# Moving the clamp of the weight decoding to GpSimd, one piece ahead, and the bonus product to VectorE

## The chip, the cores and the metric

One core of a Trainium2 chip runs the whole program. The metric is device time in microseconds (us) of one execution, the median over several. Engines are named as in the profile: PE is TensorE (PEld its weight loads), DVE is VectorE, ACT is ScalarE, POOL is GpSimd, SP is SyncE, which here only issues DMAs.

## The reference

The program is a linear attention with decay followed by two feed-forward mixers, for batch B=4, H=8 heads of D=48, S=768 steps, in fp32:

```python
cur = einsum('bhd,bhe->bhde', u[None] * kt, vt)      # bonus of the own step
y[:, :, t] = einsum('bhd,bhde->bhe', rt, state + cur)
state = w[None, :, :, None] * state + einsum('bhd,bhe->bhde', kt, vt)
...
h = maximum(x @ w_in, 0);  gate = sigmoid(conv3(h, conv_w))   # mixer 1, 384 -> 1024 -> 384
x = (h * gate) @ w_out
x + maximum(layernorm(x) * g_ln @ w_ch1, 0) @ w_ch2            # mixer 2, 384 -> 1536 -> 384
```

The weights of both mixers (w_in, conv_w, w_out, w_ch1, w_ch2) arrive as 64-bit floats, `x` of a mixer is fp32.

## The kernel before, in words

**Attention.** It works on 24 tiles of 128 steps (`attn_tile`, six a batch). A tile's keys are first multiplied by decay factors and by the bonus `u` in one DVE product (`decayed_k`, L224), which is issued two tiles ahead. Transposes on PE give `rT` (DVE L248) and `kT` (ACT L253). The bonus term of a step is the sum over d of r times k times u: the product `av` (L256, on POOL before), its sum by head `a8` (L258, DVE), and a diagonal matrix `aT` made from it by an `affine_select` (L261, POOL). Then `copy_predicated` (L271, DVE) puts the other scores of PE's `dps` into `aT`, PE makes `yps`, and L294 and L295 split it into a rounded part (ACT) and a rest (DVE). `state_update` carries the state on (L322, L324, L325 on DVE, L328 and L329 on ACT).

**Mixers.** Work goes by 8 blocks `j` of 384 steps. Every matmul of the mixers is three fp32r products (high by high, high by low, low by high). Mixer 1 has 8 slices `f` a block, with gate work on DVE (L377, L383, L396) and ACT; mixer 2 has 12 slices a block. All eight blocks of mixer 1 come first, with the attention tiles they need fed in between by `pace` (`after1`); their results go to DRAM and come back for mixer 2.

**Weight decoding.** The 22 pieces of weights (`wjobs`) come in an order written out: 0 to 2 and 4 to 6 are the halves of w_in, 512 wide; 3 and 7 to 9 are w_out, 10 to 15 w_ch1, 16 to 21 w_ch2, all 768 wide. A piece's 64-bit words are loaded by an SP DMA to `st` (three buffers), one piece ahead (`wload`). The decoding (`decode`) takes the magnitude of the high word on ACT, clamps it on DVE (`tensor_scalar` with max and min), shifts it (`tensor_scalar`), and merges the low word and then the sign (two `scalar_tensor_tensor`, "stt" below); then ACT writes the rounded part (`wih`, `woh`, `c1h`, `c2h`), and DVE the rest (`wil`, `wol`, `c1l`, `c2l`). The result of the decoding is the tile `wdec`, two buffers. All of it is recorded on line L70, that of the helper `InOrder`, which holds the operations of an engine that go through it in program order; what doesn't go through it is placed by a scheduler that plans with its own model of times.

**When a piece is decoded.** `decode` and `steps` are generators; `wdo` takes steps from them. Before, a piece has four steps with a pause behind each, and the last subtraction is joined to the next piece's first. In the start-up (four attention tiles) two steps follow each half tile, up to piece 2; in block j=0 two steps follow each of 16 slots; in j=1 to 5 every third slot has a step, in j=6 and 7 every second; in mixer 2 two steps follow each slice. `need` forces a piece to be done before the slice that uses it: in j=0 pieces 4 to 6 before f=4 and piece 7 two slices behind.

Of the kernel before, what the change touches and what calls it, by code (L numbers as in the profile page):

```python
# [8 lines left out]
F32 = mybir.dt.float32  # L9
F32R = mybir.dt.float32r  # L10
I32 = mybir.dt.int32
AF = mybir.ActivationFunctionType
ALU = mybir.AluOpType
AX = mybir.AxisListType

B, H, S, D = 4, 8, 768, 48
DM = H * D
# [3 lines left out]
NF1 = FF1 // 128  # L21
NF2 = FF2 // 128
# [21 lines left out]
def body(ctx, tc, r, k, v, w, u, w_in, conv_w, w_out, g_ln, w_ch1, w_ch2, out):  # L44
# [28 lines left out]
    vo = InOrder(nc.vector)  # L73
    ao = InOrder(nc.scalar)
    so = InOrder(nc.sync)


    ident = const.tile([128, 128], F32, name="ident")
# [25 lines left out]
    y_dram = dram.tile([B, S + 2, DM], F32, name="y_dram")  # L104


    def decode(st, n):

        words = st[:, 0:2 * n].rearrange("p (n two) -> p n two", two=2)
        lo, hi = words[:, :, 0], words[:, :, 1]  # L110
        t = ap.tile([128, WN], F32, tag="wd", name="wdec", bufs=2)[:, 0:n]
        ti = t.bitcast(I32)
        ao.activation(out=t, in_=hi.bitcast(F32), func=AF.Abs)
        vo.tensor_scalar(out=t, in0=t, scalar1=W_MIN, scalar2=W_MAX, op0=ALU.max, op1=ALU.min)
        yield
        vo.tensor_scalar(out=ti, in0=ti, scalar1=5, scalar2=2, op0=ALU.logical_shift_left,
                         op1=ALU.logical_shift_right)
        yield
        vo.scalar_tensor_tensor(out=ti, in0=lo, scalar=29, in1=ti, op0=ALU.logical_shift_right, op1=ALU.bitwise_or)
        yield  # L120
        vo.scalar_tensor_tensor(out=ti, in0=hi, scalar=-(2 ** 30), in1=ti, op0=ALU.bitwise_and, op1=ALU.bitwise_or)
        return t

    wjobs = []

    def wjob(src, n, hi, lo, scale=None):

        st = []

        def load():  # L130
            st.append(io.tile([128, 2 * WN], I32, tag="st", name="st", bufs=3))
            dst = st[0][:, 0:2 * n]
            if len(src.shape) == 3:
                dst = dst.rearrange("p (a n) -> p a n", a=src.shape[1])
            so.dma_start(out=dst, in_=src.bitcast(I32))

        def steps():
            t = yield from decode(st[0], n)
            if len(src.shape) == 3:
                t = t.rearrange("p (a n) -> p a n", a=src.shape[1])  # L140
            kw = {} if scale is None else {"scale": gl[:, scale:scale + 1]}
            ao.activation(out=hi, in_=t, func=AF.Copy, **kw)
            yield
            if scale is None:
                vo.tensor_tensor(out=lo, in0=t, in1=hi.bitcast(F32), op=ALU.subtract)
            else:
                vo.scalar_tensor_tensor(out=lo, in0=t, scalar=kw["scale"], in1=hi.bitcast(F32),
                                        op0=ALU.mult, op1=ALU.subtract)
        wjobs.append((load, steps()))
        return len(wjobs) - 1  # L150

    wi_job, wo_job, c1_job, c2_job = {}, {}, {}, {}
# [84 lines left out]
    def attn_tile(n):  # L237
        b, i = divmod(n, TPB)
        rt, kt, vt = loaded[n]
        first, last = i == 0, i == TPB - 1  # L240
        pa, pa_tag = (ps_m, "m") if n < EARLY else (ps_a, "pa")
        py, py_tag = (ps_c, "acc") if n < EARLY else (ps_a, "pa")

        prt = pa.tile([128, NP, C], F32, tag=pa_tag, name="prt")
        for p in range(NP):
            pe.transpose(prt[0:PR, p, :], rt[:, 2 * p:2 * p + 2, :].rearrange("p a d -> p (a d)")[:, 0:PR], ident)
        rT = ap.tile([PR, NP, C], F32, tag="t2", name="rT", bufs=4)
        v_.tensor_tensor(out=rT, in0=prt[0:PR], in1=tr, op=ALU.mult)  # L248
        pkt = pa.tile([128, NP, C], F32, tag=pa_tag, name="pkt")
        for p in range(NP):  # L250
            pe.transpose(pkt[0:PR, p, :], kks[:, n % 2, 0, 2 * p:2 * p + 2, :].rearrange("p a d -> p (a d)")[:, 0:PR], ident)
        kT = ap.tile([PR, NP, C], F32, tag="t2", name="kT", bufs=4)
        a_.activation(out=kT, in_=pkt[0:PR], func=AF.Copy)  # L253

        av = ap.tile([128, H, D], F32, tag="av", name="av", bufs=2)
        g_.tensor_tensor(out=av, in0=kks[:, n % 2, 1, :, 0:D], in1=rt[:, :, 0:D], op=ALU.mult)  # L256
        a8 = sp.tile([128, H, 1], F32, tag="a8", name="a8", bufs=2)
        v_.tensor_reduce(out=a8.rearrange("x (q p) o -> x q (p o)", q=2), in_=av.rearrange("x (p q) d -> x q p d", q=2),  # L258
                         axis=AX.X, op=ALU.add)
        aT = ap.tile([128, 2, NP, C], F32, tag="aT", name="aT", bufs=2)  # L260
        g_.affine_select(out=aT.rearrange("x q p c -> x (q p) c"), in_=a8.to_broadcast([128, H, C]),  # L261
                         compare_op=ALU.is_equal, fill=0.0, base=0, pattern=[[0, H], [1, C]], channel_multiplier=-1)
        yield

        dps = [ps_a.tile([128, NP, C], F32, tag="pa", name="dps") for _ in range(2)]
        for p in range(NP):
            for q in range(2):
                q0 = 64 * q
                pe.matmul(dps[q][:, p, :], lhsT=kT[q0:q0 + D, p, :], rhs=rT[q0:q0 + D, p, :], start=True, stop=True)
        for q in range(2):  # L270
            v_.copy_predicated(out=aT[:, q], mask=later.bitcast(I32), data=dps[q])  # L271
        yield

        yps = py.tile([128, KT, C], F32, tag=py_tag, name="yps")
        opened = set()

        def part(g, lhsT, rhs):
            c0 = 32 * (g % 4)
            pe.matmul(yps[c0:c0 + 32, g // 4, :], lhsT=lhsT, rhs=rhs, start=c0 not in opened, stop=True,
                      skip_group_check=True)  # L280
            opened.add(c0)

        if not first:
            for g in range(3 * NP):
                p, s_ = divmod(g, 3)
                part(g, sbd[n % 2][:, p, 32 * s_:32 * s_ + 32], rT[:, p, :])
        for parts in zip(*from_heads):
            for g, p, q, c0 in parts:
                pair = vt[:, 2 * p:2 * p + 2, :].rearrange("x a d -> x (a d)")
                part(g, pair[:, c0:c0 + 32], aT[:, q, p, :])  # L290
        j = n // TT
        xh, xl = xT[j] if j in xT else new_xT(j)
        sl = slice(1 + (n % TT) * C, 1 + (n % TT) * C + C)
        a_.activation(out=xh[:, :, sl], in_=yps, func=AF.Copy)  # L294
        v_.tensor_tensor(out=xl[:, :, sl], in0=yps, in1=xh[:, :, sl].bitcast(F32), op=ALU.subtract)  # L295
        load_tile(n + 3)
        if n + 2 < NT:
            decayed_k(n + 2)
        for t, e in ((xh, 0), (xl, 1)):
            if i == 0:  # L300
                g_.memset(t[:, :, 0:1].bitcast(F32), 0.0)
            if last:
                g_.memset(t[:, :, T + 1:T + 2].bitcast(F32), 0.0)
            if n % TT == 0 and i > 0:
                g_.tensor_copy(out=xT[j - 1][e][:, :, T + 1:T + 2], in_=t[:, :, 1:2].bitcast(F32))
                g_.tensor_copy(out=t[:, :, 0:1], in_=xT[j - 1][e][:, :, T:T + 1].bitcast(F32))
        finished[0] = n
        yield
# [321 lines left out]
        return cst  # L630

    def conv_weights(cst):
        t = yield from decode(cst, 3 * NF1)
        v_.tensor_copy(out=cw, in_=t.rearrange("p (k f) -> p k f", k=3))

    def choose_path():

        wr = sp.tile([1, DM], F32, tag="wr", name="wr", bufs=1)
        ok = sp.tile([1, 4], F32, tag="ok", name="ok", bufs=1)
        nc.sync.dma_start(out=wr, in_=w.rearrange("h d -> (h d)").unsqueeze(0))  # L640
        vo.tensor_reduce(out=ok[:, 0:1], in_=wr, axis=AX.X, op=ALU.max)
        vo.tensor_reduce(out=ok[:, 1:2], in_=wr, axis=AX.X, op=ALU.min)
        v_.tensor_scalar(out=ok[:, 2:3], in0=ok[:, 0:1], scalar1=DECAY_MAX, scalar2=None, op0=ALU.is_le)
        v_.tensor_scalar(out=ok[:, 3:4], in0=ok[:, 1:2], scalar1=DECAY_MIN, scalar2=None, op0=ALU.is_ge)
        v_.tensor_tensor(out=ok[:, 0:1], in0=ok[:, 2:3], in1=ok[:, 3:4], op=ALU.mult)
        v_.tensor_scalar(out=general, in0=ok[:, 0:1], scalar1=0.5, scalar2=None, op0=ALU.is_lt)
# [25 lines left out]
    decayed_k(0)  # L672
    while finished[0] < EARLY - 1:
        step()
        wdo(2, wi_job[0])
    for _ in conv_weights(cst):
        pass
    ahead, pace = [iter(())], [0]
    for j in range(NB):
# [10 lines left out]
        def after1(f):  # L690
# [7 lines left out]
            if j == 0:  # L698
                wdo(2, wo_job[NF1 - 1])
            elif j < NB - 2:  # L700
                wdo(slot[0] % 3 == 0, c1_job[NF2 - 1])
            else:
                wdo(slot[0] % 2 == 0, c2_job[4])
            if j == NB - 1:
                if slot[0] == 1:
                    ahead[0] = prefetch(0)
# [59 lines left out]
```

## Time and profile before

| what | value |
|---|---|
| median of 3 runs | 686.55 us (686.32 to 687.44) |
| the profiled execution | 685.54 us |
| its span, first to last instruction | 683.8 us |
| PE busy | 639.0 us (93%) |
| DVE busy | 435.1 us (64%), 822 instructions |
| ACT busy | 270.1 us (39%) |
| POOL busy | 95.0 us (14%) |
| mean granted PE clock | 0.974 |

The table gives each engine's busy time over the whole span. It is an average over unlike stretches: a start-up with few matmuls, the eight blocks of mixer 1 to about 362 us, and mixer 2 after that. The stretches are read one by one below.

### The profile page before, as it was taken

To read this page: it belongs to the slowest core of one execution; us is meant where nothing else is said; L and a number is where in the kernel's file an instruction comes from. 1 tells how busy PE (TensorE), PEld (TensorE's weight loads), DVE (VectorE), ACT (ScalarE), POOL (GpSimd) and SP (SyncE) were. 2 spreads that over 40 slices of the span, in tenths; PEclk is the share of its full clock that TensorE was granted. 3 is DMA by queue.
4 is the path that set the end of the run, shared out by engine and by line. 5 is a ranking of instruction groups with operands and counts; after the bars stand their busy time and mean duration, and the time that the engine had idled before them with its cause. 6 is when DMAs were issued, how large, how long until landed. Compare 5 with 4: busy or idle time off the path is not lost.

```text
span 683.8 us, 12373 instructions
## 1 busy us (share of the span) xinstructions
PE 639.0 (93%) x5100; PEld 609.8 (89%) x5100; DVE 435.1 (64%) x822; ACT 270.1 (39%) x537; POOL 95.0 (14%) x137
## 2 busy tenths in 40 slices
PE   3874799999999999999999999999999999999996
PEld 3764698889989978999999999999999999999995
DVE  5989899998988888997998524142332415242211
ACT  1336456556565565657675312122121212112110
POOL 6342032221212222200110000000000000000000
PEclk9887699999999999999999999999999999999999
DMA  8953542343324241403301002020201102020101
GB/s 180 180 133 78 154 107 72 86 104 82 94 71 95 57 119 22 140 1 114 130 36 59 23 1 70 1 70 1 70 1 36 34 1 70 1 69 1 35 1 39
DMA packets 93842, 45.15 MB, mean 66 GB/s; under 512 B 80337, under 2 KB 89682, under 8 KB 93778
## 3 DMA queue, kind: packets, MB, share of 16 engines
q1 hardware_dynamic: 93778, 44.28, 24.8%
q8 instruction: 42, 0.69, 0.4%
q14 instruction: 22, 0.18, 0.1%
HBM read 34.83 MB, written 9.44 MB: 65 GB/s over the span
## 4 chain that ended last, share of the span: by engine, by line
PE 54%; DVE 34%; ACT 5%; issue 3%; DMA 2%; POOL 1%; SPq 0%; ACTq 0%; DVEq 0%; POOLq 0%
PE acc L70 25%; PE psm L70 25%; DVE c L396 9%; DVE wdec L70 6%; DVE aT L271 3%; DVE gl L383 3%; DVE c L377 3%; DVE kks L224 2%; ACT c L376 1%; DVE rT L248 1%; DVE sn L325 1%; ACT c L394 1%; DVE xl L295 1%; PE pxt L70 1%; POOL av L256 1%
## 5 line engine op out<-in xcount | busy, mean ns | idle before, releaser
L410 DVE SCALAR_TENSOR_TENSOR rl<-psm,rh 128x384 fp32r<-128x384 f32 x96 | 53.3, 555 | 143.2 <-ACT rh L409 143.2
L409 ACT ACTIVATE rh<-psm 128x384 fp32r<-128x384 f32 x96 | 47.2, 491 | 212.2 <-PE psm L70 212.2
L70 PE MATMUL psm<-xnh,c1h 128*128 128x384 f32 x288 | 98.8, 343 | 0.0
L70 PE MATMUL psm<-xnh,c1l 128*128 128x384 f32 x288 | 97.5, 339 | 0.0
L70 PE MATMUL acc<-c2h,rh 128*128 128x384 f32 x288 | 97.2, 338 | 0.0
L70 PE MATMUL acc<-c2h,rl 128*128 128x384 f32 x288 | 97.2, 338 | 0.0
L70 PE MATMUL acc<-c2l,rh 128*128 128x384 f32 x288 | 97.1, 337 | 0.0
L70 PE MATMUL psm<-xnl,c1h 128*128 128x384 f32 x288 | 96.9, 336 | 0.0
L396 DVE SCALAR_TENSOR_TENSOR c<-h,cw,c 128x384 f32<-128x384 f32 x128 | 86.7, 681 | 12.0 <-ACT c L394 11.5
L70 PE MATMUL psm<-xh,wih 128*128 128x386 f32 x192 | 69.5, 362 | 8.2 <-ACT wih L70 4.7
L70 PE MATMUL acc<-woh,gh 128*128 128x384 f32 x192 | 68.2, 355 | 8.2 <-ACT woh L70 7.5
L70 PE MATMUL acc<-woh,gl 128*128 128x384 f32 x192 | 66.2, 345 | 2.0 <-DVE gl L383 1.9
L70 PE MATMUL acc<-wol,gh 128*128 128x384 f32 x192 | 65.9, 343 | 1.3 <-DVE wol L70 1.3
L70 PE MATMUL psm<-xl,wih 128*128 128x386 f32 x192 | 66.9, 348 | 0.0
L70 PE MATMUL psm<-xh,wil 128*128 128x386 f32 x192 | 66.7, 347 | 0.1
L433 POOL TENSOR_TENSOR rs<-rs,nhalf 128x1 f32<-128x1 f32 x24 | 15.6, 664 | 306.2 <-DVE rs L432 306.0
L70 PEld LDWEIGHTS psm<-xnl,c1h 128*128 128x128 f32 x288 | 54.3, 189 | 0.0
L70 PEld LDWEIGHTS psm<-xnh,c1h 128*128 128x128 f32 x288 | 54.3, 189 | 0.0
L70 PEld LDWEIGHTS psm<-xnh,c1l 128*128 128x128 f32 x288 | 54.2, 188 | 0.0
L70 PEld LDWEIGHTS acc<-c2l,rh 128*128 128x128 f32 x288 | 54.1, 188 | 0.0
L70 PEld LDWEIGHTS acc<-c2h,rh 128*128 128x128 f32 x288 | 54.1, 188 | 0.0
L70 PEld LDWEIGHTS acc<-c2h,rl 128*128 128x128 f32 x288 | 54.0, 188 | 0.0
(103 smaller groups left out, 1122.8 us busy)
## 6 DMA issues: line engine op xcount, KB each, us to landing
st<-in_moe_w_ch_dram SPq DMA_DIRECT2D x12, 768.0 KB, 5.3
rvbuf<-in_r_dram SPq DMA_DIRECT2D x24, 192.0 KB, 3.1
kt<-in_k_dram SPq DMA_DIRECT2D x24, 192.0 KB, 3.4
rvbuf<-in_v_dram SPq DMA_DIRECT2D x24, 192.0 KB, 3.1
x_dram<-x SPq DMA_DIRECT2D x24, 192.0 KB, 1.9
x1b<-x_dram SPq DMA_DIRECT2D x24, 192.0 KB, 2.9
out_dram<-x1b SPq DMA_DIRECT2D x24, 192.0 KB, 1.9
st<-in_moe_w_in_dram SPq DMA_DIRECT2D x6, 512.0 KB, 5.2
```

Source lines behind the costliest of these rows:

```text
L70: return lambda *args, **kw: tc.keep_in_program_order(op(*args, **kw))
L224: v_.tensor_tensor(out=kks[:, n % 2, :, :, 0:D], in0=loaded[n][1].unsqueeze(1).to_broadcast([128, 2, H, D]), in1=tku, op=ALU.mult)
L248: v_.tensor_tensor(out=rT, in0=prt[0:PR], in1=tr, op=ALU.mult)
L256: g_.tensor_tensor(out=av, in0=kks[:, n % 2, 1, :, 0:D], in1=rt[:, :, 0:D], op=ALU.mult)
L271: v_.copy_predicated(out=aT[:, q], mask=later.bitcast(I32), data=dps[q])
L295: v_.tensor_tensor(out=xl[:, :, sl], in0=yps, in1=xh[:, :, sl].bitcast(F32), op=ALU.subtract)
L377: v_.tensor_tensor(out=st["c"], in0=st["h"][:, 1:T + 1], in1=st["c"], op=ALU.mult)
L383: v_.tensor_tensor(out=st["gl"], in0=st["c"], in1=st["gh"].bitcast(F32), op=ALU.subtract)
L396: v_.scalar_tensor_tensor(out=c, in0=h[:, o:o + T], scalar=cw[:, tap, f:f + 1], in1=c, op0=ALU.mult, op1=ALU.add)
L409: a_.activation(out=gh, in_=ps[:, 0:T], func=AF.Relu)
L410: v_.scalar_tensor_tensor(out=gl_, in0=ps[:, 0:T], scalar=0.0, in1=gh.bitcast(F32), op0=ALU.max, op1=ALU.subtract)
L433: g_.tensor_tensor(out=rs[:, 1:2], in0=rs[:, 0:1], in1=nhalf, op=ALU.pow)
```

## The change

The clamp goes from DVE to POOL, in a function of its own (`magnitude`, with ACT's magnitude ahead of it). It is issued one piece ahead: behind the two merges of a piece, and ahead of ACT's rounded part of that piece, comes the magnitude and the clamp of the next piece, if that one's load has been issued. Both stand in program order on their engines (`ao`, `go`). The clamp's step and its pause go, so a piece has three steps; the slots are set to match (every fourth for every third, every third for every second), and the start-up decodes up to piece 3 in place of 2. The product `av` goes from POOL to DVE. The tile `wr` of `choose_path` takes a buffer of the tag `xn` in place of its own.

```diff
+    go = InOrder(nc.gpsimd)
...
+    def magnitude(st, n):
+
         t = ap.tile([128, WN], F32, tag="wd", name="wdec", bufs=2)[:, 0:n]
+        ao.activation(out=t, in_=words(st, n)[1].bitcast(F32), func=AF.Abs)
+        go.tensor_scalar(out=t, in0=t, scalar1=W_MIN, scalar2=W_MAX, op0=ALU.max, op1=ALU.min)
+        return t
+
+    def decode(st, n, t):
+
+        lo, hi = words(st, n)
         ti = t.bitcast(I32)
-        ao.activation(out=t, in_=hi.bitcast(F32), func=AF.Abs)
-        vo.tensor_scalar(out=t, in0=t, scalar1=W_MIN, scalar2=W_MAX, op0=ALU.max, op1=ALU.min)
-        yield
         vo.tensor_scalar(out=ti, in0=ti, scalar1=5, scalar2=2, op0=ALU.logical_shift_left,
                          op1=ALU.logical_shift_right)
...
+        def ahead():
+            if not mag:
+                mag.append(magnitude(st[0], n))
+
         def steps():
-            t = yield from decode(st[0], n)
+            ahead()
+            t = mag[0]
+            yield from decode(st[0], n, t)
+            if me + 1 < min(len(wjobs), w_loaded[0]):
+                wjobs[me + 1][2]()
...
-        g_.tensor_tensor(out=av, in0=kks[:, n % 2, 1, :, 0:D], in1=rt[:, :, 0:D], op=ALU.mult)
+        v_.tensor_tensor(out=av, in0=kks[:, n % 2, 1, :, 0:D], in1=rt[:, :, 0:D], op=ALU.mult)
...
-        t = yield from decode(cst, 3 * NF1)
+        t = magnitude(cst, 3 * NF1)
+        yield from decode(cst, 3 * NF1, t)
...
-        wr = sp.tile([1, DM], F32, tag="wr", name="wr", bufs=1)
+        wr = mp.tile([128, DM], F32, tag="xn", name="wr")[0:1]
...
-        wdo(2, wi_job[0])
+        wdo(2, wo_job[0])
...
-                wdo(slot[0] % 3 == 0, c1_job[NF2 - 1])
+                wdo(slot[0] % 4 == 0, c1_job[NF2 - 1])
             else:
-                wdo(slot[0] % 2 == 0, c2_job[4])
+                wdo(slot[0] % 3 == 0, c2_job[4])
```

## Rows read from the trace of the kernel before

**Rows 1.** Busy time by stretch: stretch, length, then busy us (xinstructions), PEclk, DMA share, GB/s.
```profile
0.00:102.60 102.60, 71.94 (x765) 62.24 (x766) 87.38 (x163) 43.75 (x81) 35.47 (x63) 0.83 0.61 139
102.60:362.00 259.40, 251.96 (x2519) 233.58 (x2518) 236.42 (x420) 160.99 (x327) 49.64 (x57) 1.00 0.31 81
362.00:683.00 321.00, 315.08 (x1820) 313.98 (x1819) 111.27 (x240) 65.36 (x131) 9.89 (x18) 1.00 0.10 31
```
**Rows 2.** The page's chain that ended last, by engine.
```profile
PE 54%; DVE 34%; ACT 5%; issue 3%; DMA 2%; POOL 1%; SPq 0%; ACTq 0%; DVEq 0%; POOLq 0%
```
**Rows 3.** Line L256 alone (the product av on POOL) by stretch.
```profile
0.00:102.60 102.60, 14.12 (x9) 0.83 0.61 139
102.60:362.00 259.40, 20.31 (x15) 1.00 0.31 81
```
**Rows 4.** Clamps among DVE's groups, first to 102.6 us, then 102.6 to 362.
```profile
L70 DVE TENSOR_SCALAR wdec<-wdec 128x512 f32<-128x512 f32 x6 | 3.4, 568 | 0.1
L70 DVE TENSOR_SCALAR wdec<-wdec 128x768 f32<-128x768 f32 x4 | 2.2, 557 | 0.1
...
L70 DVE TENSOR_SCALAR wdec<-wdec 128x768 f32<-128x768 f32 x9 | 5.0, 551 | 0.1
```
**Rows 5.** DVE's timeline: start us, us, engine, line, operation, tiles, shapes, count.
```profile
25.59 0.34 DVE L325 TENSOR_TENSOR sn<-sn,w 112x192 f32<-112x192 f32 x1
...
37.10 0.41 DVE L70 TENSOR_SCALAR wdec<-wdec 128x512 f32<-128x512 f32 x1
37.44 1.34 DVE L271 COPY_PREDICATED aT<-later,dps 128x512 f32<-128x512 int32 x2
...
85.92 0.56 DVE L70 TENSOR_SCALAR wdec<-wdec 128x768 f32<-128x768 f32 x1
86.39 0.55 DVE L377 TENSOR_TENSOR c<-h,c 128x384 f32<-128x384 f32 x1
86.86 0.55 DVE L70 TENSOR_SCALAR wdec<-wdec 128x768 int32<-128x768 int32 x1
```
**Rows 6.** POOL: two rows of its timeline, and one of its groups (L628).
```profile
20.24 1.10 POOL L261 TENSOR_SCALAR_AFFINE_SELECT aT<-a 128x1024 f32<-128x1024 f32 x1 [0.93 <-PE yps L70]
...
26.08 1.00 POOL L256 TENSOR_TENSOR av<-kks,rvbuf 128x384 f32<-128x384 f32 x1 [4.40 <-DVE sn L325]
...
L628 POOL TENSOR_SCALAR_AFFINE_SELECT later<-later 128x512 f32<-128x512 f32 x1 | 0.6, 634 | 0.0
```
**Rows 7.** DVE's timeline: lengthened rows, first and last beside av, first and last beside aT.
```profile
34.48 1.17 DVE L325 TENSOR_TENSOR sn<-sn,w 112x192 f32<-112x192 f32 x1
...
286.45 0.57 DVE L325 TENSOR_TENSOR sn<-sn,w 112x192 f32<-112x192 f32 x1
...
19.97 1.66 DVE L70 TENSOR_SCALAR wdec<-wdec 128x512 f32<-128x512 f32 x2
...
288.46 0.85 DVE L396 SCALAR_TENSOR_TENSOR c<-h,cw,c 128x384 f32<-128x384 f32 x1 [0.51 <-ACT c L394]
```
**Rows 8.** DVE's waits (us in total, times, longest), whole span, then to 102.6 us.
```profile
DVE a L258 <- POOL av L256: 3.6, 6, 0.9
...
DVE wil L70 <- ACT wih L70: 2.1, 3, 0.7
DVE a L258 <- POOL av L256: 1.8, 4, 0.6
```
**Rows 9.** PE's waits from 44 to 362 us, the two longest.
```profile
PE acc L70 <- ACT woh L70: 7.5, 1, 7.5
PE psm L70 <- ACT wih L70: 4.7, 2, 2.5
```
**Rows 10.** The tile st: ACT's magnitude (duration ns min/median/max), and its loads.
```profile
L70 ACT ACTIVATE wdec<-st x22: 664/896/917, 19.3 to 377.7; 128x768 f32<-128x768 f32 x16, 128x512 f32<-128x512 f32 x6
...
DMA to landing us min/median/max: 3.5/4.7/8.1
```
**Rows 11.** A piece of the chain in order of time: start us, us, what.
```profile
246.65 2.38 POOL av L256
```

More of the change, by code (lines that the diff above doesn't have):

```diff
@@ L104, in body, with words @@
     y_dram = dram.tile([B, S + 2, DM], F32, name="y_dram")
-    def decode(st, n):
-        words = st[:, 0:2 * n].rearrange("p (n two) -> p n two", two=2)
-        lo, hi = words[:, :, 0], words[:, :, 1]
+    def words(st, n):
+        return [st[:, 0:2 * n].rearrange("p (n two) -> p n two", two=2)[:, :, i] for i in range(2)]
+    def magnitude(st, n):
         t = ap.tile([128, WN], F32, tag="wd", name="wdec", bufs=2)[:, 0:n]
+        ao.activation(out=t, in_=words(st, n)[1].bitcast(F32), func=AF.Abs)
[3 more added lines that the diff above has]
+        lo, hi = words(st, n)
         ti = t.bitcast(I32)
-        ao.activation(out=t, in_=hi.bitcast(F32), func=AF.Abs)
-        vo.tensor_scalar(out=t, in0=t, scalar1=W_MIN, scalar2=W_MAX, op0=ALU.max, op1=ALU.min)
-        yield
         vo.tensor_scalar(out=ti, in0=ti, scalar1=5, scalar2=2, op0=ALU.logical_shift_left,
@@ L121, in decode @@
         vo.scalar_tensor_tensor(out=ti, in0=hi, scalar=-(2 ** 30), in1=ti, op0=ALU.bitwise_and, op1=ALU.bitwise_or)
-        return t
     wjobs = []
     def wjob(src, n, hi, lo, scale=None):
-        st = []
+        st, mag = [], []
         def load():
@@ L148, in steps @@
                                         op0=ALU.mult, op1=ALU.subtract)
-        wjobs.append((load, steps()))
+        me = len(wjobs)
+        wjobs.append((load, steps(), ahead))
         return len(wjobs) - 1
```

## The prediction

> **What bounds the kernel now.** I read the busy time by stretch first, then the chain, then DVE's waits and its timeline. There are three stretches. In the last 321 us (mixer 2) PE is busy 315 us and its weight loads 314, while DVE has 111: PE alone sets the pace, and nothing the change touches is late there [rows 1]. In the first 102.6 us it is the reverse: DVE is busy 87 us, PE 72 at a mean granted clock of 0.83, and of DVE's idle time most lies ahead of the first tiles. In the middle, 102.6 to 362 us, both are close: PE 252 of 259, its loads 234, DVE 236 [rows 1]. The chain says the same, with 54% on PE, 34% on DVE and 1% on POOL [rows 2]. So a microsecond of DVE time counts nearly whole in the first stretch, in part in the second (I take a third, since PE's own waits there are short), and not at all in the third.
>
> POOL is idle most of the time, but it isn't without a price for DVE. Where a POOL operation that reads SBUF runs, some DVE operations beside it last longer: L325 takes 0.34 us at 25.59 us, ahead of the av that starts at 26.08, but 1.17 at 34.48 beside another av [rows 5 to 7]. I went through DVE's rows against the median of their own form, with the POOL row beside each: 18 rows beside av are lengthened, by 8.6 us together, and 20 beside the affine_select, by 11.7 us; the first and last of each are [rows 7]. To 102.6 us av's part of it is 3.4 us (five rows), after that 5.2. So the two POOL operations, 48 in all and 1.0 and 1.1 us long when they run alone [rows 6], cost DVE 0.42 us each.
>
> **The change part by part.** Costs on a busy DVE go from start to start: the clamp 768 wide takes 0.47 us (85.92 to 86.39), one 512 wide 0.34 (37.10 to 37.44), and a product of two SBUF operands 128x384 also 0.47 (86.39 to 86.86) [rows 5].
>
> *Product av onto DVE.* Nine in the first stretch and 15 in the second [rows 3]: +4.2 and +7.1 us. The row used (L377) has contiguous operands, av reads runs of 48 in 64; no row shows that this matters, and L224 writes the same layout. The bounds are this 0.47 from below and the row's whole 0.55 from above, 1.9 us more over 24 [rows 5].
>
> *Clamps off DVE.* Ten in the first stretch (six 512 wide, four 768), nine in the second [rows 4]: -(6 x 0.34 + 4 x 0.47) = -3.9, and -9 x 0.47 = -4.2 us. Three more in mixer 2 count nothing. The clamp for the convolution weights, 24 wide, is left out.
>
> *POOL's av no longer in DVE's way.* -3.4 and -5.2 us, from above.
>
> *DVE no longer waits for av.* The sum a8 waited six times, 3.6 us, of which four and 1.8 us in the first stretch [rows 8]: -1.8 and -1.8. The sum now stands behind the product on its own engine. What is late next is aT on POOL, whose one operation ahead of the merge is unchanged.
>
> *Clamps on POOL.* No POOL row is a plain tensor_scalar. The nearest has one input: affine_select, 0.63 us for 512 and 1.10 for 1024 [rows 6], so about 0.86 for 768. The other end is the two-input av, 1.00 for 384 [rows 6], which would give 2.0 for 768 and 1.3 for 512. I take the nearest, 0.63 and 0.86: 6 x 0.63 + 4 x 0.86 = 7.2 us of POOL in the first stretch, 7.7 in the second. The time on POOL itself is free, since the result is wanted a piece later; behind the clamp in POOL's queue stand aT and the casts, at most 0.86 us later, and those wait seldom on the chain. The price is DVE's lengthening. For the affine_select it was 11.7 us over 24 x 1.1 = 26 us, a share of 0.45; by that the clamps cost 3.3 and 3.5 us. The ends: nothing, and the whole 7.2 and 7.7 us.
>
> *One piece ahead, and the even decoding in block 0.* Before, pieces 4 to 7 are decoded in one burst near 72 to 85 us, where PE waits 4.7 us for wih and 7.5 for woh [rows 9] and DVE itself 0.7 three times for ACT's rounded part [rows 8]. With three steps a piece and piece 3 done in the start-up, block 0 reaches f=4 with these done. DVE's work is the same, so PE's wait buys little by itself; I take half of the two late 0.7 us waits, -0.7 us. The magnitude of the next piece now stands ahead of this piece's rounded part on ACT, and needs a load that lands 4.7 us after issue (8.1 at most) [rows 10]; in block 0 that is about two slots, so it can hold ACT up for a microsecond, behind it kT and the gate work. I set it to nothing, with 3 us as the other end. Piece 3 in the start-up moves about 3 us of DVE work ahead of the first mixer matmul and out of block 0: no net. Piece 4's load moves with it into SP's queue among the loads of r, k and v; these are issued three tiles ahead, which hides it, and at worst one landing of 4.7 us is seen [rows 10]. wr's DMA now waits for an xn buffer late in mixer 1, in front of a stretch where DVE has room: nothing, or one short landing, 3.5 us [rows 10], if DVE's two reductions come to stand waiting for it ahead of mixer 2's first slices.
>
> The sum: first stretch 4.2 - 3.9 - 3.4 - 1.8 + 3.3 - 0.7 = -2.3 us, counted whole; second 7.1 - 4.2 - 5.2 - 1.8 + 3.5 = -0.6, a third of it -0.2. Together -2.5 us. The profiled execution took 685.54 us and would take 683.0; it lies 1.0 us under the median shown, which would go from 686.55 to 684.0.
>
> **A page against this change.** The lengthened rows show a POOL operation and a DVE operation that exclude one another for a time: 1.17 us for 0.34 is nearly the whole of an av [rows 5 to 7]. The Trainium skill has the rule for it in "SBUF — State Buffer", section "SBUF: two separate sides": the port pair of these two engines is an exclusive lock held for a whole instruction, and the loser fully blocks; the trace agrees row by row. "Perfetto Trace Analysis", section "Optimizing Scalar/DVE Operations", also of the Trainium skill, draws from it that moving operations between DVE and GPSIMD might not help. By that rule at its hardest, every clamp stops DVE for all its length, which is the first rival; the trace bears it out in part only, since the 48 POOL operations cost 0.42 us each and not 1.0.
>
> **The rivals.** *First, slower: the clamps block DVE whole.* In block 0 and the bursts DVE has little but operations with two SBUF operands, and the clamp is issued right beside the merges. Then the first stretch pays 7.2 in place of 3.3, the second a third of 7.7 in place of a third of 3.5: +3.9 + 1.4, net +2.8 us, 689.4. It decides from a share of 0.45 + 2.5 / (7.2 + 7.7 / 3) = 0.71 upward. For it: single rows lengthened by a whole POOL operation [rows 7]. Against it: the mean share of 0.45. Chance 0.20.
>
> *Second, no change: 686.5.* The DVE time saved is spent as waits elsewhere, the matmuls of the first blocks being paced by ACT and by PE's lower clock, and the first mixer matmul starting later behind piece 3. For it: PE is near its limit in the middle stretch [rows 1]. Against: DVE's 87 us of the first 102.6. Chance 0.17.
>
> *Third, a larger gain.* PE's 12.2 us of waiting for weights in block 0 [rows 9] falls by a third, because slices get done early and leave less for the PE-bound middle, and av's place on the chain (2.38 us at 246.65) [rows 11] goes too. That is some -6 us, 680.5. Against: DVE has no idle time to pay for it. Chance 0.13.
>
> *Fourth, the clamp isn't ahead in effect.* If ACT is held by the load, or the clamp waits behind aT, DVE's shift waits for magnitude and clamp as before, now on two other engines; ten pieces at some 0.75 us in the first stretch make +7.5, net +5, 691.5. For it: the load's 4.7 us. Against: the three buffers and the long slots. Chance 0.08.
>
> **How the numbers follow.** The forecast has 0.42. About 1.4 us, 0.2%, is what a measurement here can tell from no change. The forecast's own spread of 2 to 3 us puts four fifths of it on the faster side; with the third rival and a little of the second that is 0.49. The second rival mostly, and the edges of forecast and first, give 0.20 for no change. The first, the fourth and the forecast's lower edge give 0.31. The range reaches from beyond the third rival's place, 678, to short of the fourth's, 691; the planner places other operations anew, and no row bounds that.
>
> **What would show it.** Right: av on DVE at 0.55 us each, POOL's tensor_scalar near 0.86 and 0.63, no a8 wait for av, no L325 row beyond 0.4 us, DVE's lengthening by clamps about 7 us, and the weight waits of PE in block 0 gone. Wrong: clamps at 1.3 us or more, stt rows (wdec) lengthened by a whole clamp each, DVE waiting for the clamp, or ACT waiting for the load of st ahead of a rounded part.

## The result and the profile after

The changed kernel takes 680.91 us (median of four, 680.11 to 681.52) against 687.00 beside it (686.32 to 688.38): a ratio of 0.9908 [0.9888, 0.9929], 6.1 us less where the prediction had 2.5. The direction was right, and 680.91 lies inside the range; the size was more than twice the forecast. The profiled execution took 680.46 us, its span 678.7, the mean granted clock 0.977.

The busy time of the changed kernel by stretch (columns as in [rows 1]; the last stretch ends earlier, with the span):

```profile
0.00:102.60 102.60, 71.07 (x792) 61.12 (x792) 88.89 (x168) 46.90 (x86) 48.00 (x66) 0.87 0.64 143
102.60:362.00 259.40, 252.83 (x2518) 236.66 (x2519) 236.52 (x412) 159.37 (x327) 56.17 (x47) 1.00 0.31 81
362.00:678.00 316.00, 310.41 (x1793) 309.01 (x1791) 109.29 (x244) 62.66 (x125) 18.93 (x23) 0.99 0.09 30
```

PE gets through 792 matmuls in the first stretch, 765 before; the granted clock's mean is 0.87, 0.83 before; POOL has more to do. DVE's whole busy time, though, is the same to 0.4 us (434.7, before 435.1), so the gain can't be read from that sum. The chain that ended last has moved from DVE to PE (before: 54% and 34% [rows 2]):

```profile
PE 62%; DVE 26%; ACT 4%; issue 3%; DMA 2%; POOL 1%; SPq 0%; DVEq 0%; POOLq 0%
```

Where the time went is best read from PE, whose matmuls come in the same order in both kernels, so that one and the same matmul can be looked up in both. The first of mixer 1 (`psm`, L70) starts at 44.55 us before and at 49.47 after: the start-up is 4.9 us **longer**. The first slice of block 1 is taken over by ACT (`h`) at 104.80 before and 101.34 after. The first is before, the second after:

```profile
104.80 0.47 ACT L393 ACTIVATE h<-psm 128x386 f32<-128x386 f32 x1
```
```profile
101.34 0.49 ACT L407 ACTIVATE h<-psm 128x386 f32<-128x386 f32 x1 [0.90 <-PE pst L70]
```

That is 3.5 us ahead, so block 0 took some 8 us less. The last such slice of mixer 1 is 5.8 us ahead (362.0 and 356.2), the end 5.1. So about 3.5 us come by block 1 and 2.3 in blocks 1 to 7; mixer 2 gives nothing, as predicted.

The largest change in block 0 stands in PE's timeline at the first down matmul (`acc`, of piece 3, the first of w_out). Before:

```profile
58.25 0.33 PE L70 MATMUL psm<-xh,wil 128*128 128x386 f32 x1
...
66.10 0.69 PE L70 MATMUL acc<-woh,gh 128*128 128x384 f32 x1 [7.52 <-ACT woh L70]
...
68.09 0.69 PE L70 MATMUL acc<-wol,gh 128*128 128x384 f32 x1 [1.30 <-DVE wol L70]
68.57 0.52 PE L70 MATMUL acc<-woh,gl 128*128 128x384 f32 x1
68.89 0.52 PE L70 MATMUL acc<-woh,gh 128*128 128x384 f32 x1
```

and after:

```profile
62.05 0.34 PE L70 MATMUL psm<-xh,wil 128*128 128x386 f32 x1
62.23 0.34 PE L70 MATMUL acc<-woh,gh 128*128 128x384 f32 x1
62.40 0.34 PE L70 MATMUL acc<-wol,gh 128*128 128x384 f32 x1
64.43 0.44 PE L70 MATMUL acc<-woh,gl 128*128 128x384 f32 x1 [1.70 <-DVE gl L397]
```

The waits of 7.52 us for piece 3's rounded part and of 1.30 for its rest are gone, and one of 1.70 for the gate's `gl` has come. Before, the matmuls behind the waits took 0.52 to 0.69 us each, 0.32 apart, and PE's granted clock was 0.50 from 66 to 72 us (1.00 from 55 to 60): the lower of its two levels, 1.2 GHz, after the stop. After, they take 0.34 us, 0.17 apart, at a clock of 1.00 (58 to 64 us). DVE is busy 13.5 of the 14 us from 58 to 72 before, and all of them after, so PE's stop alone doesn't say what block 0 lost. PE's longest waits from 44 to 362 us, which answer to [rows 9]:

```profile
PE psm L70 <- ACT wih L70: 7.8, 2, 5.2
PE prt L70 <- DVE aT L285: 3.7, 5, 1.1
PE dps L70 <- DVE rT L262: 2.8, 2, 2.7
PE psm L70 <- POOL xl L315: 2.8, 1, 2.8
```

So PE's waits for weights went from 12.2 to 7.8 us: `woh` is gone, `wih` is 3.1 longer.

On DVE and POOL, the groups of the changed kernel that the prediction spoke of (L270 is the product av, L339 was L325, L410 was L396):

```profile
L270 DVE TENSOR_TENSOR av<-kks,rvbuf 128x384 f32<-128x384 f32 x24 | 13.0, 547 | 0.0
...
L339 DVE TENSOR_TENSOR sn<-sn,w 112x192 f32<-112x192 f32 x16 | 5.5, 347 | 0.0
...
L410 DVE SCALAR_TENSOR_TENSOR c<-h,cw,c 128x384 f32<-128x384 f32 x128 | 84.5, 661 | 9.1 <-ACT c L408 8.1
```
```profile
L70 POOL TENSOR_SCALAR wdec<-wdec 128x768 f32<-128x768 f32 x16 | 48.4, 3024 | 98.7 <-ACT wdec L70 85.0 <-DVE c L410 13.6
L70 POOL TENSOR_SCALAR wdec<-wdec 128x512 f32<-128x512 f32 x6 | 14.1, 2350 | 16.4 <-ACT wdec L70 8.5 <-DVE c L410 4.6 <-PE yps L70 3.3
```

The product costs its 0.55 us, L339's mean is 347 ns (L325's was 658 before), and no wait of the sum for av is left. The clamp, though, takes 3.02 and 2.35 us on POOL, where the prediction had 0.86 and 0.63. That it costs DVE far less than that is seen beside one clamp, on POOL's timeline and on DVE's:

```profile
130.27 3.02 POOL L70 TENSOR_SCALAR wdec<-wdec 128x768 f32<-128x768 f32 x1 [4.26 <-ACT wdec L70]
```
```profile
129.57 0.61 DVE L410 SCALAR_TENSOR_TENSOR c<-h,cw,c 128x384 f32<-128x384 f32 x1
130.10 0.55 DVE L270 TENSOR_TENSOR av<-kks,rvbuf 128x384 f32<-128x384 f32 x1
130.57 1.18 DVE L410 SCALAR_TENSOR_TENSOR c<-h,cw,c 128x384 f32<-128x384 f32 x1
131.67 0.54 DVE L272 TENSOR_REDUCE a<-av 128x8 f32<-128x384 f32 x1
132.13 1.00 DVE L70 SCALAR_TENSOR_TENSOR c1l<-wdec,gl,c1h 128x768 fp32r<-128x768 f32 x1
133.06 0.55 DVE L391 TENSOR_TENSOR c<-h,c 128x384 f32<-128x384 f32 x1
```

Only the operation at its start is lengthened, 1.18 us for 0.61; the three behind it run at their usual durations beside a clamp that goes on for 1.6 us more. Counting DVE's rows against the median of their own form, with the POOL row beside each, all 23 clamps lengthen 11 rows by 5.4 us in sum; the affine_select lengthens 19 by 14.1. With 0.4 beside a cast that is 19.9 in all; before, affine_select and av together made 20.3 (11.7 and 8.6). The relief from av was used up by the clamps and by the affine_select.

### The profile page after: what moved, and what is told of

It is laid out like the page before. It is cut to its first block, busy times and chain, and to the rows that moved or that the text cites. A ratio compares the mean times of both kernels' runs of the same rounds, so it can differ in the third digit from the quotient of the medians.

```text
span 678.7 us, 12382 instructions
## 1 busy us (share of the span) xinstructions
PE 634.3 (93%) x5100; PEld 606.8 (89%) x5100; DVE 434.7 (64%) x823; ACT 268.9 (40%) x537; POOL 123.1 (18%) x136
## 4 chain that ended last, share of the span: by engine, by line
PE 62%; DVE 26%; ACT 4%; issue 3%; DMA 2%; POOL 1%; SPq 0%; DVEq 0%; POOLq 0%
PE psm L70 28%; PE acc L70 28%; DVE c L410 6%; DVE wdec L70 4%; DVE aT L285 3%; DVE gl L397 3%; DVE c L391 2%; PE yps L70 2%; DMA x1b<-x_dram 2%; PE dps L70 1%; DVE rT L262 1%; PE pxt L70 1%; POOL wdec L70 1%; DVE av L270 1%; DVE kks L238 1%
## 5 line engine op out<-in xcount | busy, mean ns | idle before, releaser
L70 PE MATMUL psm<-xnh,c1h 128*128 128x384 f32 x288 | 99.0, 344 | 0.1
L70 PE MATMUL psm<-xnh,c1l 128*128 128x384 f32 x288 | 97.5, 338 | 0.0
L70 PE MATMUL acc<-c2h,rh 128*128 128x384 f32 x288 | 97.1, 337 | 0.0
L70 PE MATMUL acc<-c2l,rh 128*128 128x384 f32 x288 | 97.1, 337 | 0.0
L70 PE MATMUL acc<-c2h,rl 128*128 128x384 f32 x288 | 97.0, 337 | 0.0
L70 PE MATMUL psm<-xnl,c1h 128*128 128x384 f32 x288 | 96.9, 337 | 0.0
L410 DVE SCALAR_TENSOR_TENSOR c<-h,cw,c 128x384 f32<-128x384 f32 x128 | 84.5, 661 | 9.1 <-ACT c L408 8.1
L70 POOL TENSOR_SCALAR wdec<-wdec 128x768 f32<-128x768 f32 (+2 forms) x23 | 62.8, 2729 | 115.2 <-ACT wdec L70 93.6
L70 PE MATMUL psm<-xh,wih 128*128 128x386 f32 x192 | 68.9, 359 | 10.7 <-ACT wih L70 7.8
L70 PE MATMUL acc<-woh,gh 128*128 128x384 f32 x192 | 67.4, 351 | 2.3 <-DVE xl L309 1.5
L70 PE MATMUL acc<-woh,gl 128*128 128x384 f32 x192 | 65.6, 341 | 2.7 <-DVE gl L397 2.7
L70 PE MATMUL psm<-xl,wih 128*128 128x386 f32 x192 | 66.2, 345 | 0.0
L70 PE MATMUL psm<-xh,wil 128*128 128x386 f32 x192 | 66.2, 345 | 0.0
L70 PE MATMUL acc<-wol,gh 128*128 128x384 f32 x192 | 65.2, 340 | 0.0
L390 ACT ACTIVATE c<-c 128x384 f32<-128x384 f32 x64 | 33.5, 524 | 56.2 <-DVE c L410 56.0
L70 PEld LDWEIGHTS psm<-xnh,c1h 128*128 128x128 f32 x288 | 54.3, 189 | 0.4 <-DVE ok L658 0.4
L70 PEld LDWEIGHTS psm<-xnl,c1h 128*128 128x128 f32 x288 | 54.4, 189 | 0.0
L70 PEld LDWEIGHTS psm<-xnh,c1l 128*128 128x128 f32 x288 | 54.2, 188 | 0.0
L70 PEld LDWEIGHTS acc<-c2l,rh 128*128 128x128 f32 x288 | 54.1, 188 | 0.0
```

The source lines that it names most:

```text
L70: return lambda *args, **kw: tc.keep_in_program_order(op(*args, **kw))
L390: a_.activation(out=st["c"], in_=st["c"], func=AF.Sigmoid)
L410: v_.scalar_tensor_tensor(out=c, in0=h[:, o:o + T], scalar=cw[:, tap, f:f + 1], in1=c, op0=ALU.mult, op1=ALU.add)
```

## Experiments

Ratios are to the kernel before, run beside each, with their 95% intervals. Where two variants are compared, their ratios are subtracted and multiplied by 687 us.

**One part alone.** The question is which part makes the gain: av's move, piece 3 in the start-up, the clamp's leaving DVE, or its being ahead.

The kernel before with piece 3 in the start-up, and nothing else:

```diff
-        wdo(2, wi_job[0])
+        wdo(2, wo_job[0])
```

> The kernel before with one line changed: the start-up decodes up to piece 3. Schedule theory (the gain of the change is piece 3 decoded ahead of the first block): PE's 7.5 us wait for woh near 58 us goes, the first mixer matmul starts 2 to 4 us later, and the time falls by 3 to 6 us, to 681 to 684. Port theory (the gain is that av left POOL, so DVE is no longer lengthened and no longer waits): no change, 686 to 688. Clamp theory (the gain is the clamp on POOL a piece ahead): no change either.

684.11 us, 0.9948 [0.9934, 0.9963]: -3.6 us, where the prediction had no net. In the trace, one of each kernel, PE's stop is not what went, though. The first mixer matmul starts at 44.94 us (before 44.55), PE waits for the gate instead of the weights at the first down matmul,

```profile
PE acc L70 <- ACT gh L382: 5.6, 1, 5.6
```

and with 0.9 more for `gl` it stops for 6.5 us there, 8.8 before. The first slice of block 1 is only 0.3 us ahead (104.5), the last of mixer 1 is 3.0 (359.0). DVE's rows are lengthened by 17.2 us in this trace, 20.3 before, which is as much; that this is the cause was not tried.

The kernel before with av on DVE, and nothing else:

```diff
-        g_.tensor_tensor(out=av, in0=kks[:, n % 2, 1, :, 0:D], in1=rt[:, :, 0:D], op=ALU.mult)
+        v_.tensor_tensor(out=av, in0=kks[:, n % 2, 1, :, 0:D], in1=rt[:, :, 0:D], op=ALU.mult)
```

> The kernel before with the product av on DVE alone. Schedule theory: within 1.5 us of the kernel before, since DVE pays 11.3 us for the product and gets back 8.6 us of lengthening and 3.6 us of waits. Port theory: 3 to 6 us faster, 681 to 684. Clamp theory: no change.

683.06 us, 0.9937 [0.9923, 0.9951]: -4.3 us, where av's terms in the prediction's sum give -1.0.

The changed kernel with av put back on POOL:

```diff
-        v_.tensor_tensor(out=av, in0=kks[:, n % 2, 1, :, 0:D], in1=rt[:, :, 0:D], op=ALU.mult)
+        g_.tensor_tensor(out=av, in0=kks[:, n % 2, 1, :, 0:D], in1=rt[:, :, 0:D], op=ALU.mult)
```

> The changed kernel with av back on POOL. Schedule theory: within 1.5 us of the changed kernel, 680 to 682.5; POOL then holds av, clamp and affine_select, and av may stand behind a clamp of 2.8 us, so a loss is likelier than a gain. Port theory: 4 us or more slower than the changed kernel, 685 or more.

685.82 us, 0.9988 [0.9973, 1.0004]. Without av's move next to nothing of the change's gain is left; DVE's rows are lengthened by 24.7 us here. From the other end av's move is worth 5.5 us, with the clamp's lateness in it: av and clamp now share POOL, and DVE waits 4.2 us for clamps, 0.8 in the changed kernel.

The changed kernel with the clamp on DVE, still one piece ahead (av in one buffer instead of two):

```diff
-        go.tensor_scalar(out=t, in0=t, scalar1=W_MIN, scalar2=W_MAX, op0=ALU.max, op1=ALU.min)
+        vo.tensor_scalar(out=t, in0=t, scalar1=W_MIN, scalar2=W_MAX, op0=ALU.max, op1=ALU.min)
```

> The changed kernel with the clamp on DVE, still a piece ahead and with three steps (av in one buffer instead of two, so that it fits). Schedule theory: within 1.5 us of the changed kernel, since 8 us of clamps on DVE stand against 5.4 us of lengthening. Clamp theory: 3 us or more slower than the changed kernel, 684 or more.

679.56 us, 0.9892 [0.9875, 0.9908], 1.1 us under the changed kernel by the ratios, with overlapping intervals. Moving the clamp gained nothing; whether it lost a microsecond is not told apart. The rival that its leaving DVE makes the gain falls.

**The two parts together, and the clamp not ahead.** The kernel before with its clamp on POOL, in the old place:

```diff
-        vo.tensor_scalar(out=t, in0=t, scalar1=W_MIN, scalar2=W_MAX, op0=ALU.max, op1=ALU.min)
+        go.tensor_scalar(out=t, in0=t, scalar1=W_MIN, scalar2=W_MAX, op0=ALU.max, op1=ALU.min)
```

> The kernel before with the clamp on POOL in its old place: four steps, not ahead. In the changed kernel the clamp takes 2.8 us on POOL (768 wide). Theory that being ahead is what pays: DVE's shift waits for magnitude and clamp in each piece wherever pieces follow one another, 3 to 10 us slower than before, 690 or more. Rival, that the planner puts other work between: within 1.5 us of before, 686 to 688.5.

690.93 us, 1.006 [1.004, 1.008]: 4.1 us slower. With av still on POOL, DVE's rows are lengthened by 27.2 us, and DVE waits for the clamp:

```profile
DVE wdec L70 <- POOL wdec L70: 3.3, 5, 1.3
```

In the changed kernel that wait is 0.8 us, once. So being ahead takes away a wait that the move to POOL itself brings. The 4.1 us are not the price of that wait alone: DVE's rows are lengthened by 7 us more than before.

Both diffs of the first two variants together:

> The kernel before with av on DVE and piece 3 in the start-up, and nothing else: clamp on DVE, four steps, old slots. If the two edits add and the rest of the change (one piece ahead, three steps, slots) is worth nothing: 0.9948 x 0.9937 = 0.9885 of before, 679 to 680.5, as the changed kernel with the clamp on DVE. If the rest is worth something: 681.5 or more. If both edits remove the same wait: 682.5 or more.

681.49 us, 0.9910 [0.9892, 0.9928]: two lines of the change, with nothing done to the decoding, give the whole of it within the intervals. Beside av's move piece 3 is worth 1.9 us, not 3.6. What is left for one piece ahead, three steps and the thinner slots together (against the variant with the clamp on DVE) is 1.2 us with overlapping intervals: that stays open.

av on DVE, and piece 3 forced to be done ahead of the first slice of block 0 instead of being decoded in the start-up, so that only its place in the program differs:

```diff
+            if f == 0:
+                need(wo_job[0])
```

> The kernel before with av on DVE and piece 3 forced to be done at slice 0 of block 0, behind the start-up instead of in it. Theory that piece 3 is best decoded while DVE waits for the first mixer matmuls (2.3 us idle there): the first mixer matmul stays at 45 us, PE's wait for woh falls below 2 us, and the time is 2 us or more under that of the kernel with av on DVE and piece 3 in the start-up: 676 to 678. Rival, that DVE's sum alone decides up to 100 us: the same as that kernel within 1 us, 679 to 681.

681.13 us, 0.9906 [0.9889, 0.9924], the same as with piece 3 in the start-up. In the traces the piece hardly moves, either: ACT's rounded part ends at 52.3 us here and at 50.6 there, DVE's rest at 55.7 and 58.0. So this doesn't tell whether its place matters; in both it is done by the first down matmul.

**Why av's move is worth so much.** It does two things: it takes a POOL operation from beside DVE, and it gives DVE a product. First POOL's part, in two ways. The same product made by POOL as well, with av on DVE (POOL's copy is not used; it goes to a part of aT ahead of the affine_select, which overwrites it):

```diff
-        g_.tensor_tensor(out=av, in0=kks[:, n % 2, 1, :, 0:D], in1=rt[:, :, 0:D], op=ALU.mult)
+        v_.tensor_tensor(out=av, in0=kks[:, n % 2, 1, :, 0:D], in1=rt[:, :, 0:D], op=ALU.mult)
...
+        g_.tensor_tensor(out=aT[:, 0, 0:3, :].rearrange("x p c -> x (p c)").rearrange("x (h d) -> x h d", h=H), in0=kks[:, n % 2, 1, :, 0:D], in1=rt[:, :, 0:D], op=ALU.mult)
```

> av on DVE as in the kernel with that edit alone, and POOL makes the same product too, into a part of aT that the affine_select then overwrites; nothing reads it. Port theory (av on POOL cost time because it lengthens DVE's operations): 3 to 5 us slower than with av on DVE alone, 686 to 688. Wait theory (it cost time because the sum a8 came late): within 1.5 us of av on DVE alone, 682 to 684.5.

696.44 us, 1.0128 [1.0107, 1.0148]: 13.1 us more than with av on DVE alone, where 3 to 5 were expected. But this product can hold up aT, so the rival that aT's lateness makes the cost was not yet excluded. The same product behind the affine_select, into a tile that nobody reads, where it delays no aT of its own tile (both stand in program order on POOL, av has one buffer):

```diff
+        spare = ap.tile([128, H, D], F32, tag="spare", name="spare", bufs=1)
+        go.tensor_tensor(out=spare, in0=kks[:, n % 2, 1, :, 0:D], in1=rt[:, :, 0:D], op=ALU.mult)
```

> av on DVE, and POOL makes the same product too, into a tile that nothing reads, but ordered behind the affine_select of its tile, so that aT isn't held up by it (in the run with the product ahead of aT the loss was 13 us). If the port alone makes the loss, by lengthened DVE operations: 8 us or more slower than av on DVE alone, 691 or more. If aT's lateness made most of it: 1 to 5 us slower, 684 to 688.

694.49 us, 1.0123 [1.0105, 1.0142], 12.8 us more than with av on DVE alone by the ratios (11.4 by the medians, which stand beside different runs of the kernel before). DVE's rows are lengthened by 25.8 us against 14.9 there. The same line of the gate work, with av on DVE alone and then with the spare product too:

```profile
L396 DVE SCALAR_TENSOR_TENSOR c<-h,cw,c 128x384 f32<-128x384 f32 x128 | 86.3, 677 | 8.5 <-ACT c L394 7.8
```
```profile
L399 DVE SCALAR_TENSOR_TENSOR c<-h,cw,c 128x384 f32<-128x384 f32 x128 | 91.8, 720 | 9.2 <-ACT c L397 8.5
```

By the end of ACT's row of the first slice of block 1 this costs 0.9 us (104.2 against 103.3), by that of the last slice of mixer 1 10.6 (369.1 against 358.5). So 9.7 us arise in blocks 1 to 7, where DVE's rows are lengthened by 9.5: in the stretch that the prediction counted by a third, a lengthened microsecond cost a whole one. DVE's idle time there is the same in both traces (16.5 and 16.3 us). PE's waits grow with it, those for aT, two merges later, from 2.0 to 4.7 us, those for `xl` from 2.9 to 8.4. They may be the way there or a cost of their own: that the product holds up what stands behind it in POOL's queue (the next aT, the edges of `xl`) is not excluded.

Then DVE's part: av on DVE, made twice into the same tile (the second repeats the first; av in one buffer, `wr` in an `xn` buffer as in the change):

```diff
+        v_.tensor_tensor(out=av, in0=kks[:, n % 2, 1, :, 0:D], in1=rt[:, :, 0:D], op=ALU.mult)
```

> av on DVE as in the kernel with that edit alone, and made twice there, the second time over the first. It prices DVE's time: 24 x 0.47 = 11.3 us more of it, 4.2 of them in the first 102.6 us. If DVE's time counts whole everywhere in mixer 1: 11 us slower than av on DVE alone, 694. If whole in the first stretch and a third behind it, as the prediction had it: 6.6 us slower, 689.5. If it counts in the first stretch only: 4 us slower, 687.

690.43 us, 1.0058 [1.0042, 1.0075]: 8.3 us more by the ratios, 7.4 by the medians, for 24 x 0.47 = 11.3 us of DVE work, some 0.7 a microsecond: 1.8 us by the start of block 1 (105.1 against 103.3, ends of ACT's row as above), where nine products make 4.2, and 4.7 more by the end of mixer 1 (365.0 against 358.5), where fifteen make 7.1. The prediction's weighting would make 6.6 us of this, near the sum, by another split.

The two together make -12 + 8 = -4, and -4.3 was measured. That they meet is luck in part, for the trace with av's move alone is made up otherwise. Up to the last slice of mixer 1 (start 362.0 us before, 358.0 with av on DVE) DVE is busy 4.5 us longer (328.3 against 323.8) and idle 8.5 less (29.7 against 38.2). The lengthening has fallen by 5.4 only: the 8.6 beside av are gone, but the affine_select lengthens by 14.8 where it was 11.7. Of the idle time, 3.6 us are the wait for av; 4.8 are shorter waits for ACT's `c`, before and with av on DVE, to 362 us:

```profile
DVE c L396 <- ACT c L394: 11.1, 14, 2.3
DVE c L377 <- ACT c L376: 8.1, 15, 0.6
```
```profile
DVE c L396 <- ACT c L394: 7.8, 9, 2.3
DVE c L377 <- ACT c L376: 6.6, 12, 0.6
```

Why ACT keeps DVE waiting less is not settled.

**What the clamp's length costs.** The changed kernel with the upper limit left out:

```diff
-        go.tensor_scalar(out=t, in0=t, scalar1=W_MIN, scalar2=W_MAX, op0=ALU.max, op1=ALU.min)
+        go.tensor_scalar(out=t, in0=t, scalar1=W_MIN, scalar2=None, op0=ALU.max)
```

> The changed kernel with the clamp's upper limit left out, so one operation in place of two (inputs stay below the limit). It shows what sets the 2.8 us of the clamp on POOL. If POOL pays by operation: 1.5 us or less at 768 wide. If by element and not by operation: 2.8 us still. The time of the kernel: within 1.5 us of the changed kernel in both cases, since a clamp holds DVE up for 0.9 us at most, whatever it lasts.

```profile
L70 POOL TENSOR_SCALAR wdec<-wdec 128x768 f32<-128x768 f32 x16 | 38.1, 2380 | 101.2 <-ACT wdec L70 86.9 <-DVE c L410 14.3
L70 POOL TENSOR_SCALAR wdec<-wdec 128x512 f32<-128x512 f32 x6 | 11.5, 1921 | 16.9 <-ACT wdec L70 12.3 <-DVE c L410 4.6
```

Neither of the two durations expected came, but one between (their 2.8 us is the mean over both widths; 768 wide it was 3.02). The kernel takes 680.34 us, 0.9912 [0.9888, 0.9935], the same as the changed kernel. The clamps are 12.9 us shorter in sum (62.5 to 49.6), and neither the time nor what they take from DVE (5.7 us against 5.4) goes down: what a clamp lasts beyond the one row that it lengthens is free here.

**A faster version.** If what POOL takes from DVE is the matter, the affine_select is the next to go, with 14 us. The variant with the clamp on DVE, and aT built by ACT, eight copies of the identity a tile, each scaled by its column of a8:

```diff
-        g_.affine_select(out=aT.rearrange("x q p c -> x (q p) c"), in_=a8.to_broadcast([128, H, C]),
-                         compare_op=ALU.is_equal, fill=0.0, base=0, pattern=[[0, H], [1, C]], channel_multiplier=-1)
+        for h in range(H):
+            a_.activation(out=aT[:, h // NP, h % NP, :], in_=ident, func=AF.Copy, scale=a8[:, h])
```

> The changed kernel with the clamp on DVE, and the diagonal matrix aT made by ACT, as eight scaled copies of the identity, in place of POOL's affine_select. POOL then reads nothing large beside DVE, and DVE's 14 us of lengthening go; ACT gets 24 x 8 copies of 0.25 us or so, 48 us, in a stretch where it is busy 60%. If the port is what costs: 4 us or more faster than with the affine_select, 676 or less. If ACT's chain (h, c, sigmoid, gh) gets late instead: slower, 682 or more.

671.47 us (671.04 to 671.76), 0.9780 [0.9763, 0.9797]: faster than both kernels, 7.7 us by the ratios under the variant that it started from. In its groups, the 192 copies on ACT and L410 again; the latter had a mean of 694 ns in that variant:

```profile
L276 ACT ACTIVATE aT<-ident,a 128x128 f32<-128x128 f32 x192 | 58.8, 390 | 3.5 <-DVE a L272 3.5
...
L410 DVE SCALAR_TENSOR_TENSOR c<-h,cw,c 128x384 f32<-128x384 f32 x128 | 78.3, 614 | 9.9 <-ACT c L408 9.1
```

No row of DVE is lengthened by POOL any more (14.0 us in the variant that it started from). ACT has 58.8 us more to do (0.39 us a copy, where 0.25 was expected), and the time still falls: ACT had the room (40% of the span busy in the changed kernel, 61% from 102.6 to 362 us). PE's waits for aT, 2.8 us in that variant, are gone as well, so the 7.7 us are not shown to come from the lengthening alone. The last slice of mixer 1 starts at 346.4 us, against 354.9.

## Why the prediction was off

The prediction's sum of -2.5 and the runs, part by part, in us (measured by differences of ratios along a chain of variants, so that they add up to the whole, -6.3):

| part | predicted | measured |
|---|---|---|
| av off POOL and onto DVE, a8's wait gone | -1.0 | -4.3 |
| piece 3 in the start-up | 0 | -1.9 |
| one piece ahead, three steps, slots | -0.7 | -1.2, open |
| clamps off DVE and onto POOL | -0.8 | +1.1, open |

**One weight by stretch for all of DVE's time failed.** The step said that a microsecond of DVE time counts "nearly whole in the first stretch, in part in the second (I take a third, since PE's own waits there are short)", and it counted products added, rows lengthened and waits alike. By the runs they differ. The product made twice cost 0.4 of its time up to block 1 and two thirds of it in blocks 1 to 7 (4.7 us for 7.1); beside the spare product a lengthened microsecond cost a whole one there. A larger third for everything would not have mended it: with the second stretch counted whole, av's terms make -1.0 + 0.1 = -0.9, since product and relief nearly cancel there. Short waits of PE, 97% busy there in the mean, don't say that DVE has slack: each short wait may end on it.

The terms of av were not all right either. The wait for av, 3.6 us, went as forecast. The relief from lengthening, 8.6, was 5.4 in the trace of av's move alone, since the affine_select took 3.1 more. And the sum has no term for DVE's waits for ACT's `c`, which fell by 4.8. By these runs a lengthened microsecond weighs more than an added one, unless POOL's queue has a part in it; why is not settled, nor why the waits for `c` got shorter.

**Piece 3 was set to "no net", and PE's wait was put at the wrong piece.** The prediction placed the 7.5 us wait for `woh` in "one burst near 72 to 85 us", pieces 4 to 7. It stands at 58.25 to 66.10 us and is for piece 3. The row in [rows 9] has no time of its own; the timeline has. Alone, piece 3 in the start-up is worth 3.6 us, beside av's move 1.9. What it does is not what the wait suggests, and stays open: alone, it leaves PE a stop of 6.5 us at the same matmul, for the gate, and most of the gain comes in blocks 1 to 7. Nor did the 3 us of decoding move ahead of the first mixer matmul there: that starts 0.4 us later, and `wol` of piece 3 is written from 59.85 us on. In the changed kernel, where a piece has three steps, `wol` is done at 49.37, and the start-up is 4.9 us longer.

**The clamp on POOL: wrong in duration, nearly right in price.** 0.86 and 0.63 us were taken from the nearest one-input row, and 3.02 and 2.35 came, beyond the far end of 2.0 and 1.3 too. What they cost DVE, 5.4 us, is close to the 6.8 predicted (3.3 + 3.5), since a clamp lengthens at most one row of DVE, by about 0.6 us; with the clamps' 8.1 us off DVE that still made a small gain, where the runs show none. The first rival had each clamp stop DVE for its whole length. The rule that the prediction named beside it, in the Trainium skill's "SBUF — State Buffer", section "SBUF: two separate sides", has the lock held for a whole instruction. The affine_select fits this (1.10 us alone, and most rows that it lengthens are 0.8 to 1.0 us longer), the clamp doesn't: of 3.02 us about 0.6 were seen at 130.57, and three DVE operations ran on beside the rest, two of them with two operands in SBUF. The measurement decides, and the rival falls.

**The other rivals.** The third was the nearest, 680.5 us, and named what happened: PE's weight waits of 12.2 us fell by a third, to 7.8. That its number came out is luck in part: it gave 4 us to those waits and 2.4 to av, and the variants have 1.9 for piece 3 and 4.3 for av. "Against: DVE has no idle time to pay for it" was wrong: DVE is idle 38.2 us before the last slice of mixer 1, and 35.9 in the changed kernel. The fourth (the clamp not ahead in effect) did not come; with the clamp in its old place on POOL the kernel was 4.1 us slower, lengthening included. The second, no change, is in its number what the changed kernel comes to with av left on POOL. Right were av at 0.55 us, no wait for av, L325 back to 0.35, nothing in mixer 2, and no visible price for the load order or for `wr`'s new place; these last two were not tried by themselves.

## What to carry to other kernels

A POOL operation is priced by what it does to DVE's rows beside it, row against median, and by who waits for it, and not by its own length. Such lengthening can count whole even at a PE busy share of 97%: 9.7 us for 9.5 beside the spare product, though 7.7 for 14.0 where the affine_select went. A sum of two prices measured apart should be held against the trace of the move itself, DVE's busy and idle time up to the same matmul, before it is believed. Moving such work to an engine with room (here ACT) can pay although it costs more engine time there: 192 copies, 58.8 us of ACT, made the kernel 7.7 us faster. And a long wait in a list of waits must be looked up in the timeline before it is given to a piece of work, and is no gain by itself: here it was for another piece, and when that was moved, a wait for the gate took most of its place.

## What the runs showed of the hardware

POOL's tensor_scalar with max and min took 3.02 us for 128x768 fp32 in the mean, with max alone 2.38, while its affine_select took 1.10 for 128x1024 alone [rows 6]: the two kinds don't scale from one another. Eleven of the 23 clamps lengthened one DVE row each, by 0.2 to 0.6 us; beside the clamp at 130.27 us the three rows behind it ran at their usual durations. The affine_select lengthened 19 rows, most by 0.8 to 1.0 us. PE came back from 7.5 us of waiting with matmuls of 0.52 to 0.69 us at a granted clock of 0.50 (1.2 GHz), where without the wait they took 0.34 at 1.00. ACT's scaled copy of 128x128 took 0.39 us.
